# Forward transforms that fold mirrored time rows in a rotated basis, with the mirrored rows gathered by index and the row blocks normalised one at a time

## The chip, the cores and the metric

The kernel runs on one core of one Trainium2 chip. The metric is device time in microseconds (us) of one execution. A run counts as fast or slow by its distance from the fastest run of the same kernel (over 1.5% is slow), and comparisons below use fast runs alone.

Engine names are those of the profile: PE is the tensor engine, PEld its weight loads, DVE VectorE, ACT ScalarE, POOL GpSimd, SP the engine whose queue issues most DMA transfers.

## The reference, cut to what matters

```python
def _A_ref(q, k, v, shift_k, ssm_k, ssm_D):        # S = 2048 rows, D = 640 channels, bf16
    k_shift = sum over 4 taps t of k_pad[:, t:t + S, :] * shift_k[:, 3 - t]
    kv = k_shift * v
    y = irfft(rfft(kv, 2 * S) * rfft(ssm_k, 2 * S))[:S]   # causal convolution along time
    return q * (y + kv * ssm_D)

def _B_ref(x, w1, b1, w2, b2):
    h = _layernorm(x)                                # per row, over 640 channels
    u = gelu(einsum("bsd,sf->bdf", h, w1) + b1)      # F = 1536; contracts over time
    return transpose(einsum("bdf,fs->bds", u, w2) + b2)

g = sigmoid((q * gate_w).sum(-1))
out = g * _A_ref(q, k, v, ...) + (1 - g) * _B_ref(q, ...)
```

Both halves need the same `q`. Part B (the "MLP" below) is 2 x 384 matmuls of 320 columns. Part A is a convolution computed with forward transforms of `ssm_k` (called W, two halves of the time axis) and of `kv` (called A, two halves), a product, and inverse transforms. MLP matmuls have no partner that they must wait for once their rows of X are normalised, so the kernel uses them as filler on PE wherever part A makes PE wait.

## The kernel before

A small list scheduler written in the kernel orders every operation on its engine by a model of durations. `.after` adds an edge to that model only: it shapes the order and is not a wait at run time. Waits at run time come from the data that an operation reads and writes. `dma(..., chain=True)` puts transfers on the SP queue in the given order. `tt` and `ts` are tensor-tensor and tensor-scalar operations on the named engine, and `act` is an ACT operation that empties the PE accumulator into SBUF.

```python
        def k_turn(hk):                      # k rows -> transposed k, for the 4-tap shift
            o, i = kp[hk % 2], kn[hk % 2]
            # ... ov, iv: views that regroup channels
            SC.add("DVE", 0.75, ... tensor_copy(ov, iv) ..., prio=0, name="kperm")
            c0 = 16 + 128 * (hk % 2)
            dma(KT[hk // 2][:, :, c0:c0 + 128], o[:, :, :], ..., transpose=True, chain=True)
# ... loads and the transform basis: integer angles on DVE, Sin on ACT ...
        def fwd(src, h, p, dst, slot, scale, name, neg=...):     # 64 matmuls, 16 evictions per transform
            for k2 in range(2):
                for c in range(2):
                    # ...
                    for kt in range(2):
                        for ci in range(2):
                            items.append((chk(ci), FTB[:, p, kt, c, k2, :], src(kt, p, ci), kt == 0, kt == 1))
                    mms(vt, items, name=name)
                    act(o, two, ACT.Copy, vt=vt, name=name + "e", **kw)
# ... mixing: six DVE operations of 2560 to 5120 elements a transform ...
        def ln_apply():
            ts("POOL", sd[:, :], mv[:, :, 1], 1e-5, None, ALU.add)
            tt("POOL", rstd[:, :], sd[:, :], V(cst, 1, [[0, 16]]), ALU.pow)
            tt("POOL", sd[:, :], sd[:, :], rstd[:, :], ALU.mult)
            for t in range(16):
                xs = X[:, t // 4, t % 4, :]
                ts("DVE", xs, xs, mv[:, t, 0:1], rstd[:, t:t + 1], ALU.subtract, ALU.mult, mode=4, extra=0.16)
# ...
            if h == 0:
                # ... statistics of the 16 row tiles (ln_tile, DVE) ...
                ln_apply()
                for g0 in (0, 10):           # KF: the taps spread out, the other operand of the kv matmuls
                    tt("POOL", KF[:, g0:g0 + 10, :, :], V(cw, ...), V(m32, ...), ALU.mult)
                for hk in range(2):
                    k_turn(hk)
                mixing(C[0], SS, 0, fine=True)
            else:
                mixing(C[1], C[0], 0, conj=True)
# ... v loads, second pair of k rows, their k_turn, next w1 chunk: all on the SP queue in this order ...
        def v1mix(Wh, Ws, Vh, Vs):           # part of the mixing of W, done by accumulating transfers
            for i in range(2):
                dma(V(Vh, ...), V(Wh, ...), 128 * 5120 * 2, stream="POOL", prio=0, accum=True)
        v1mix(C[0], 2, C[1], 2)
        v1mix(SS, 0, C[0], 0)
# ... kv(hk): 40 matmuls KF x KT a quarter, ACT eviction, DVE product with v; then fwd of kv, mixing ...
```

## Time and profile before

| | before |
|---|---|
| time, median of 3 runs | 192.68 us (192.67 to 192.70) |
| span of the profiled run | 190.9 us |
| PE, DVE, ACT, POOL busy | 177.4, 170.3, 116.4, 33.0 us |
| PE idle (span less busy) | 13.5 us |
| X normalised (16 operations) | 30.05 to 35.84 us |
| first kv matmuls | 41.77 us |
| PE unbroken | from 51.75 us on |

From the page of the kernel before: engines with busy time, its share of the span and the number of instructions; two rows of the forty slices (a digit is the busy share of a slice in tenths; PEclk is the clock granted to PE); and the chain of waits that ended last.

```profile
PE 177.4 (93%) x1403; PEld 130.5 (68%) x1403; DVE 170.3 (89%) x195; ACT 116.4 (61%) x187; POOL 33.0 (17%) x29
PE   0749989999799999999999999999999999999993
...
PEclk9999999999999999999999999999999999999999
...
PE 71%; DVE 19%; DMA 4%; POOL 2%; issue 2%; SPq 0%; ACT 0%; DVEq 0%
PE pp L293 71%; DVE stats L845 6%; DMA X<-in_A_q_dram 4%; DVE X L628 3%; DVE SS L617 3%; DVE C L617 2%; DVE kp L724 2%; POOL rstd L617 2%; DVE vkv L617 1%; DVE mv L847 1%; POOL sd L627 1%; SPq L267 0%; ACT O L655 0%; DVE O L617 0%; DVEq L187 0%
```

PE is busy 93% of the time, the granted clock drops in no slice, and most of the chain is PE itself. What a change of the transforms can win must come out of PE's work or its idle 13.5 us.

The timeline of DVE and then of POOL before (start, duration, engine, line, operation, shapes, count, and in brackets the idle time before and its releaser).

```profile
21.58 0.82 DVE L724 COPY kp<-kn 128x2560 bf16<-128x2560 bf16 x1
...
24.56 0.83 DVE L724 COPY kp<-kn 128x2560 bf16<-128x2560 bf16 x1
...
30.05 5.79 DVE L628 TENSOR_SCALAR X<-X,mv,rstd 128x640 bf16<-128x640 bf16 x16 [3.19 <-POOL rstd L617]
```

```profile
13.65 7.84 POOL L617 TENSOR_TENSOR KF<-cw,m 128x2240 bf16<-128x2240 bf16 x2 [5.40 <-DVE mv L847]
25.60 1.39 POOL L627 TENSOR_SCALAR sd<-mv 128x16 f32<-128x16 f32 x1 [4.11 <-DVE mv L847]
27.07 2.94 POOL L617 TENSOR_TENSOR rstd<-sd,cst 128x16 f32<-128x16 f32 x1
```

Sixteen normalisations take 5.79 us.

Second, the SP queue and POOL's own transfers before.

```profile
48.19 6.34 SPq L260 DMA_TRANSPOSE KT<-kp  x2
```

### The profile page before, as it was taken

To read this page: it belongs to the slowest core of one execution; us is meant where nothing else is said; L and a number is where in the kernel's file an instruction comes from. 1 tells how busy PE (TensorE), PEld (TensorE's weight loads), DVE (VectorE), ACT (ScalarE), POOL (GpSimd) and SP (SyncE) were. 2 spreads that over 40 slices of the span, in tenths; PEclk is the share of its full clock that TensorE was granted. 3 is DMA by queue.
4 is the path that set the end of the run, shared out by engine and by line. 5 is a ranking of instruction groups with operands and counts; after the bars stand their busy time and mean duration, and the time that the engine had idled before them with its cause. 6 is when DMAs were issued, how large, how long until landed. Compare 5 with 4: busy or idle time off the path is not lost.

```text
span 190.9 us, 3358 instructions
## 1 busy us (share of the span) xinstructions
PE 177.4 (93%) x1403; PEld 130.5 (68%) x1403; DVE 170.3 (89%) x195; ACT 116.4 (61%) x187; POOL 33.0 (17%) x29
## 2 busy tenths in 40 slices
PE   0749989999799999999999999999999999999993
PEld 0536555678566976767777777888888777886782
DVE  7999967999999799999999969999999958999451
ACT  4799997889599999998411221131322467516632
POOL 2619563600006300010012102250000000000000
PEclk9999999999999999999999999999999999999999
DMA  5999999993799999994368914999947903210222
GB/s 155 327 412 378 372 238 230 307 407 136 136 181 306 250 232 306 272 329 96 59 138 251 231 27 138 272 208 195 263 136 224 367 18 137 72 69 2 72 103 103
DMA packets 37296, 38.93 MB, mean 204 GB/s; under 512 B 15644, under 2 KB 32673, under 8 KB 37281
## 3 DMA queue, kind: packets, MB, share of 16 engines
q1 hardware_dynamic: 34464, 32.15, 54.7%
q0 software_dynamic: 2752, 6.55, 18.6%
q8 instruction: 11, 0.18, 0.4%
q14 instruction: 5, 0.03, 0.0%
q10 hardware_dynamic: 64, 0.01, 0.0%
HBM read 25.87 MB, written 2.62 MB: 149 GB/s over the span
## 4 chain that ended last, share of the span: by engine, by line
PE 71%; DVE 19%; DMA 4%; POOL 2%; issue 2%; SPq 0%; ACT 0%; DVEq 0%
PE pp L293 71%; DVE stats L845 6%; DMA X<-in_A_q_dram 4%; DVE X L628 3%; DVE SS L617 3%; DVE C L617 2%; DVE kp L724 2%; POOL rstd L617 2%; DVE vkv L617 1%; DVE mv L847 1%; POOL sd L627 1%; SPq L267 0%; ACT O L655 0%; DVE O L617 0%; DVEq L187 0%
## 5 line engine op out<-in xcount | busy, mean ns | idle before, releaser
L293 PE MATMUL pp<-X,ring 128*128 128x320 bf16 x384 | 54.0, 299 | 0.1
L293 PE MATMUL pp<-GT,W 128*128 128x320 bf16 x384 | 52.8, 299 | 0.0
L617 DVE TENSOR_TENSOR C<-C 128x2560 bf16<-128x2560 bf16 (+1 forms) x28 | 48.9, 1769 | 1.2 <-ACT C L655 1.1
L293 PEld LDWEIGHTS pp<-GT,W 128*128 128x128 bf16 x384 | 43.5, 113 | 8.9 <-ACT cgb L655 0.2
L293 PEld LDWEIGHTS pp<-X,ring 128*128 128x128 bf16 x384 | 37.1, 98 | 15.4 <-DVE X L628 0.7
L655 ACT ACTIVATE C<-pp 128x640 bf16<-128x640 f32 x64 | 39.6, 741 | 4.4 <-PE pp L293 4.3
L655 ACT ACTIVATE O<-pp,c,omg 128x640 bf16<-128x640 f32 (+1 forms) x17 | 14.5, 853 | 32.9 <-PE pp L293 32.9
L655 ACT ACTIVATE GT<-pp,cc 128x640 bf16<-128x640 f32 x12 | 9.6, 797 | 22.1 <-PE pp L293 21.9
L617 DVE TENSOR_TENSOR tm<-C,C 128x2560 bf16<-128x2560 bf16 (+2 forms) x12 | 20.2, 1708 | 1.9 <-DMA C<-tm 1.9
L293 PE MATMUL pp<-wT,FTB 128*128 128x320 bf16 x128 | 19.6, 310 | 0.6 <-ACT wT L655 0.4
L655 ACT ACTIVATE cgb<-pp,gg 128x640 bf16<-128x640 f32 x16 | 12.7, 793 | 7.7 <-PE pp L293 7.7
L293 PEld LDWEIGHTS pp<-wT,FTB 128*128 128x128 bf16 x128 | 11.5, 101 | 8.0 <-ACT C L655 2.3
L617 DVE TENSOR_TENSOR C<-tm 128x2560 bf16<-128x2560 bf16 (+1 forms) x12 | 15.0, 1263 | 0.1
L293 PE MATMUL pp<-ident,ssm 128*128 128x128 bf16 x80 | 8.8, 265 | 6.6 <-DMA ssm<-in_A_ssm_k_dram 5.3
L262 POOL DMA_DIRECT2D C<-C x6 | 7.5, 1407 | 36.0 <-DVE C L617 36.0
L845 DVE BATCH_NORM_STATS2 stats<-X 128x6 f32<-128x320 bf16 x32 | 13.4, 463 | 0.3 <-DMA X<-in_A_q_dram 0.3
L293 PE MATMUL pp<-C,GTB 128*128 128x320 bf16 x96 | 13.6, 299 | 0.0
L293 PEld LDWEIGHTS pp<-ident,ssm 128*128 128x128 bf16 x80 | 6.3, 127 | 9.1 <-DMA ssm<-in_A_ssm_k_dram 5.3
L293 PEld LDWEIGHTS pp<-C,GTB 128*128 128x128 bf16 x96 | 9.0, 98 | 4.0 <-ACT O L655 0.2
L655 ACT ACTIVATE gq<-gq 128x640 bf16<-128x640 bf16 x16 | 11.8, 756 | 0.0
L617 DVE TENSOR_TENSOR tm<-C,SS 128x5120 bf16<-128x5120 bf16 x4 | 11.2, 2817 | 0.0
L655 ACT ACTIVATE wT<-pp 128x640 bf16<-128x640 f32 x16 | 10.1, 812 | 1.1 <-PE pp L293 1.1
(64 smaller groups left out, 177.2 us busy)
## 6 DMA issues: line engine op xcount, KB each, us to landing
ring<-in_B_w_dram SPq DMA_DIRECT2D x12, 512.0 KB, 10.3
W<-in_B_w_dram SPq DMA_DIRECT2D x8, 768.0 KB, 7.3
C<-C POOLq DMA_DIRECT2D x6, 640.0 KB, 10.5
ssm<-in_A_ssm_k_dram SPq DMA_DIRECT2D x4, 640.0 KB, 9.1
X<-in_A_q_dram SPq DMA_DIRECT2D x4, 640.0 KB, 9.5
kn<-in_A_k_dram SPq DMA_DIRECT2D x4, 640.0 KB, 9.2
out_dram<-O SPq DMA_DIRECT2D x7, 320.0 KB, 2.3
vkv<-in_A_v_dram SPq DMA_DIRECT2D x2, 640.0 KB, 4.7
```

Of the source, the lines that this page charges most:

```text
L262: ins = engobj.dma_start(out_ap, in_ap, accum_op=ALU.add, max_dma_last_dim=2560)
L293: ins = self.nc.tensor.matmul(ps_ap, lhsT=lhsT, rhs=rhs, start=start, stop=stop, skip_group_check=True)
L617: return SC.add(eng, d, lambda s: T.op(eng, lambda e: e.tensor_tensor(o, a, b, op), [a, b], [o]), [a, b], [o], prio=prio, name="tt")
L627: return e.tensor_scalar(o, a, s1, None, op0=op0)
L628: return e.tensor_scalar(o, a, s1, s2, op0=op0, op1=op1)
L655: return T.op("ACT", lambda e: e.activation(o, src, func, **kw), rr + [src], ww)
L724: SC.add("DVE", 0.75, lambda s: T.op("DVE", lambda e: e.tensor_copy(ov, iv), [i[:, :, :]], [o[:, :, :]]), [i[:, :, :]], [o[:, :, :]], prio ...
L845: SC.add("DVE", 0.38, (lambda o, i: lambda s: T.op("DVE", lambda e: e.bn_stats(o, i), [i], [o]))(o, i), [i], [o])
L847: SC.add("DVE", 0.12, (lambda o, i: lambda s: T.op("DVE", lambda e: e.bn_aggr(o, i), [i], [o]))(o, i), [i], [o])
```

## The change

Its intent is to do less. A time row and its mirror (row 1024 - n) meet the same cosine up to sign and the same sine up to sign. If the rows are first folded (sum and difference with the mirrored row), the second stage of the transform is partly done before the matmuls, so a transform needs 56 matmuls instead of 64 and the mixing on DVE loses two operations of 2560 elements. The price is that every second block of rows must arrive in reverse: `k` and `v` rows are gathered by an index, `ssm_k` is reversed by copies. The folds of W are done by accumulating signed transposes on PE, those of kv on DVE. The rotated basis is no longer its own transposed inverse, so the inverse basis is built again late (integer angles, Sin). And the normalisation is cut into four blocks so that MLP filler can begin sooner. The core of the diff, with cuts:

```diff
 # loads: odd blocks reversed by a gathered load issued from POOL
+        def block_load(t, off, src, h, e):
+            o = V(t, off, [[1, 4 * D]])
+            if e:
+                dma(o, dr(src, 0, [[4 * D, S // 4], [1, 4 * D]]), 128 * 5120, stream="POOL", rows=bidx[:, h:h + 1])
+            else:
+                dma(o, dr(src, 1024 * h * D, [[4 * D, 128], [1, 4 * D]]), 128 * 5120, chain=True)
 ...
+        for hk in range(1, 4):
+            w1_load(0, hk)
         for hk in range(2):
             k_load(hk)
-        for hk in range(4):
-            w1_load(0, hk)
 ...
+        def turn(h, d0, nd, eng="POOL"):      # reversal copies of ssm_k
+            o, i = ssmR[h][:, d0:d0 + nd, :, :], V(ssm, ... [[1024, nd], [1, 4], [-4, 128]])
+            return SC.add(eng, ..., tensor_copy(o, i), ..., name="turn")
 ...
-        def mixing(R, Th, Ts, fine=False, conj=False):
+        def mixing(R, Th, Ts, conj=False):
 ...
-            tt("DVE", sl(R, 2), sl(Th, Ts), sl(Th, Ts + 1), ALU.add)
-            tt("DVE", sl(R, 3), sl(Th, Ts), sl(Th, Ts + 1), ALU.subtract)
+            tt("DVE", sl(R, 2), sl(Th, Ts), sl(R, 3), ALU.add)
+            tt("DVE", sl(R, 3), sl(Th, Ts), sl(R, 3), ALU.subtract)
 ...
-        def ln_apply():
-            ts("POOL", sd[:, :], mv[:, :, 1], 1e-5, None, ALU.add)
-            tt("POOL", rstd[:, :], sd[:, :], V(cst, 1, [[0, 16]]), ALU.pow)
-            tt("POOL", sd[:, :], sd[:, :], rstd[:, :], ALU.mult)
-            for t in range(16):
+        def ln_scale(hk):
+            a, b = 4 * hk, 4 * hk + 4
+            ts("POOL", sd[:, a:b], mv[:, a:b, 1], 1e-5, None, ALU.add, prio=0)
+            tt("POOL", rstd[:, a:b], sd[:, a:b], V(cst, 1, [[0, 4]]), ALU.pow, prio=0)
+            return tt("POOL", sd[:, a:b], sd[:, a:b], rstd[:, a:b], ALU.mult, prio=0)
+
+        def ln_apply(hk):
+            for t in range(4 * hk, 4 * hk + 4):
 ...
-                ln_apply()
-                for g0 in (0, 10):
-                    tt("POOL", KF[:, g0:g0 + 10, :, :], ...)
+                    lnlast = ln_scale(hk)
+                    if hk:
+                        ln_apply(hk - 1)
+                ln_apply(3)
                 for hk in range(2):
                     k_turn(hk)
 ...
+        for g0 in (0, 10):
+            tt("POOL", KF[:, g0:g0 + 10, :, :], ...).after.update((turn1, lnlast))
 ...
-                    128 * 5120 * 2, stream="POOL", prio=0, accum=True)
+                    128 * 5120 * 2, stream="POOL", prio=0, accum=True).after.update(kturns)
 ...
-        for p in range(4):
-            dma(GTB[...], FTB[...], 128 * 2048, rate=200.0, transpose=True, prio=10 ** 5)
+        for p in (0, 2, 1, 3):                # inverse basis: 16 integer operations, 4 masks, 4 Sin
+            ...
```

## The prediction

> **What bounds the kernel now.** The tensor engine. The page gives PE 177.4 of 190.9 us busy; DVE 170.3, ACT 116.4. The chain of waits is one unbroken PE run from 51.75 to 187.81 us; before 51.75 it runs through DVE (normalisation statistics, a wait for GpSimd's power, mixing). The timeline shows MLP matmuls filling every gap from 30.64 us on, when the first of X is normalised. PE's "busy" before that is partly padding: the first 64 W-transform matmuls take 10.29 us (161 ns each, against 137 to 141 ns for MLP ones) because each group of four waits for a 0.60 us ACT eviction; 35 transposes take 3.96 us (113 ns) at the pace of 0.63 us evictions, though five weight loads take 0.32 us (64 ns). At 64 ns a transpose and 138 ns a 320-column matmul, PE needs about 15.5 us of work between 5.3 and 30.6 us: some 10 us is recoverable, plus a 1.04 us wait for the kv product at 50.7.
>
> **What the change does (estimates from those durations).**
> - Transforms: 64 to 56 matmuls each, four transforms: 32 x 0.14 = 4.5 us less PE.
> - W transposes: 80 to 140 (folding by accumulated signed transposes): +60 x 0.064 = 3.8 us. PE demand: about -0.7 us net.
> - ACT evictions: same number (64 + 16), so the W stage stays bound by ACT until about 41 us. Fewer matmuls there only make room for MLP filler.
> - DVE: mixing loses two 2560-element operations per transform, -8 x 1.4 = 11 us. Added: folds of kv about 2 x 2.1; the inverse basis built by 16 integer operations and four masks, about 6.7; reversal copies and small items about 2.5. Forward angles: about -1. Net -1 to +2 us busy, but the 3.2 us DVE wait for the power (idle before X) goes.
> - GpSimd: gains reversal copies, four normalisation chains, three halo copies (the one now took 2.9 us), gathered loads[...]. Its chain ts 1.39, power 2.94, multiply 0.22 may shrink little with size, so four could cost 10 to 18 us.
> - ACT: four late Sin calls (1.15 us each) among Gelus need table loads (1.28 each in this trace[...]). ACT waits 3.5 us per Gelu there, so little harm. Four basis transposes by DMA go.
>
> **On the critical path.** The gain is not the fewer matmuls but normalised X arriving by blocks (estimate 17, 22, 27, 32 us instead of all by 35.8), so MLP filler uses PE while ACT evicts: 4 to 5 us of the 10. The first transposes wait for the reversal, about 1 to 2 us lost. Late, inverse matmuls end at 180.02 with 7.8 us of MLP filler left, so DVE doesn't bind if its net is as above; PE savings reach the end.
>
> **Predicted: 188.0 us, 80% range 184.0 to 192.5.** Chances: faster by over 2% 0.57, within 2% 0.37, slower 0.06.
>
> **Checks.** PE busy 172 to 176; first MLP matmul before 25 us; W stage still ends near 41; no PE gap after 52 us; inverse transforms ending well before the last MLP matmuls; table loads 4 to 8.
>
> **What would make it wrong.** GpSimd: if its queue holds up the second transpose or the power, PE idles before 30 us and the gain vanishes. Gathered loads are issued by GpSimd[...]; GpSimd-issued accumulations here took 10 to 18 us to land against 9 for ordinary loads, so late k or v rows could starve the kv stage beyond the MLP filler of the first weight chunk. Or the inverse basis comes late and table loads stall Gelu's eviction. On the other side, near-perfect filling would give about 184.

## More of the kernel before

The two KF products on POOL (13.65 to 21.49) run beside the statistics, not beside the normalisations.

```profile
57.02 2.64 POOL L262 DMA_DIRECT2D C<-C  x2 [19.65 <-DVE C L617]
61.34 2.43 POOL L262 DMA_DIRECT2D C<-SS  x2 [1.68 <-DVE C L617]
```

The second pair of k transposes is issued from 48.19 to 54.53 us; the accumulating transfers of W's mixing come after it, from 57.02 us. The k transposes land in 4.9 to 9.7 us, with a median of 5.0: this second pair in 5.0 and 4.9, and the 9.7 is the first transpose of all, issued at 22.42 us while w1 loads are still in flight.

## The result and the profile after

The ratios below are the mean time of one kernel's fast runs over the mean of the other's fast runs of the same rounds, so they are not quite the ratio of the quoted medians.

| | before | after |
|---|---|---|
| time, median | 192.69 us (192.67 to 192.75) | 205.44 us (202.65 to 207.62) |
| ratio of fast runs | 1 | 1.0577, interval 1.0474 to 1.068 |
| span of the profiled (fast) run | 190.9 us | 202.8 us |
| PE busy, PE idle | 177.4, 13.5 us | 179.8, 23.0 us |
| DVE, ACT, POOL busy | 170.3, 116.4, 33.0 us | 183.1, 130.9, 43.3 us |
| last of X normalised | 35.84 us | 41.58 us |
| first kv matmuls | 41.77 us | 53.05 us |
| PE unbroken from | 51.75 us | 95.38 us |

The kernel is 5.8% slower; as two of its four runs count as slow by the 1.5% rule, this rests on the other two (202.65 and 204.98 us, mean 203.8). The span grew by 11.9 us: 9.5 us more PE idle time (23.0 less 13.5) and 2.4 us more PE busy time (179.8 less 177.4), although PE has less to do. By PE's waits, the 9.5 us are mainly 4.7 us for X and 2.6 us for the halo copies (edge columns of k that POOL copies next to their neighbours), neither of which PE waited for before, then about 1 us more at the start and 0.9 us more for the kv product. The page of the kernel after, the same lines as before:

```profile
PE 179.8 (89%) x1431; PEld 133.2 (66%) x1431; DVE 183.1 (90%) x234; ACT 130.9 (65%) x198; POOL 43.3 (21%) x51
PE   1199999289996994989999999999999999999993
...
PEclk9999999958998899999999999999999999999999
...
PE 52%; DVE 25%; DMA 10%; ACT 8%; POOL 3%; issue 2%; SPq 0%; POOLq 0%; DVEq 0%
PE pp L296 52%; DVE X L640 7%; DVE stats L895 6%; DMA KT<-kp 5%; DMA kn<-in_A_k_dram 5%; ACT gq L667 3%; DVE C L629 3%; DVE pint L640 3%; ACT ksh L667 2%; ACT C L667 1%; DVE vkv L629 1%; POOL KT L952 1%; DVE mv L897 1%; DVE ssmR L827 1%; DVE kp L744 1%
```

A slice is 5.07 us. PE has a new hole around 36 to 41 us (digit 2), after which the clock falls to half for a slice, and smaller ones at 62 to 64 us (digit 6; the clock dips again) and 76.7 to 79.6 us (digit 4). Three names on the chain are new or larger: "DVE X" at 7% (3% before), and "DMA KT<-kp" and "DMA kn" at 5% each (absent before). The first two turned out to be the causes; the third follows from the first, as is shown below. The timeline of DVE after, then of POOL:

```profile
18.42 3.36 DVE L640 TENSOR_SCALAR X<-X,mv,rstd 128x640 bf16<-128x640 bf16 x1
...
30.71 0.81 DVE L744 COPY kp<-kn 128x2560 bf16<-128x2560 bf16 x1
...
32.81 8.77 DVE L640 TENSOR_SCALAR X<-X,mv,rstd 128x640 bf16<-128x640 bf16 x4 [0.58 <-POOL rstd L629]
41.50 1.48 DVE L629 TENSOR_TENSOR SS<-C 128x2560 bf16<-128x2560 bf16 x1
...
44.42 0.82 DVE L744 COPY kp<-kn 128x2560 bf16<-128x2560 bf16 x1
```

```profile
18.96 2.62 POOL L827 COPY ssmR<-ssm 128x1536 bf16<-128x1536 bf16 x2
...
33.00 8.04 POOL L629 TENSOR_TENSOR KF<-cw,m 128x2240 bf16<-128x2240 bf16 x2
```

The last four normalisations take 8.77 us where four took 1.45 before (5.79 for 16). In the same 8 us POOL does its two KF products, 4.02 us each, and the slowest single normalisation of the run took 4.07 us. In the first block already, a normalisation of 3.36 us lies beside the reversal copies on POOL. The chain of waits then goes on: mixing at 41.50, and the k copy that began at 24.56 before now begins at 44.42. PE during this:

```profile
37.29 0.45 PE L296 MATMUL pp<-X,ring 128*128 128x320 bf16 x2 [1.13 <-DVE X L640]
41.28 1.25 PE L296 MATMUL pp<-X,ring 128*128 128x320 bf16 x4 [3.54 <-DVE X L640]
...
63.98 3.73 PE L296 MATMUL pp<-vkv,FTB 128*128 128x320 bf16 x14 [1.97 <-DVE vkv L629]
```

The four matmuls at 41.28 take as long as eight do elsewhere (1.25 us): the granted clock was 0.50 from 41.28 to 46.5 us (0.66 in the whole stretch 40 to 50 us). Before it lie 4.67 us of waits in 36 to 41.3 us, 3.54 of them in one piece. A shorter wait was followed by half clock too: after the 1.97 us before 63.98 the granted clock was 0.52 from 64 to 66 us, and the 14 matmuls there took 266 ns each; and in e13 (below), after one of 2.52 us, eight matmuls took 1.78 us and the next six 1.80. The waits of 1.49 and 1.15 us before 78.14 and 79.57 us were not followed by it: the granted clock was 1.00 from 79.57 to 90 us. What decides it was not isolated.

The SP queue after, and POOL's transfers:

```profile
31.54 16.67 SPq L261 DMA_TRANSPOSE KT<-kp  x2
...
48.88 0.43 SPq L270 DMA_DIRECT2D kn<-in_A_k_dram  x1
...
59.65 11.70 SPq L261 DMA_TRANSPOSE KT<-kp  x2
```

```profile
56.67 1.32 POOL L265 DMA_DIRECT2D C<-C  x1 [3.86 <-DVE C L629]
62.73 1.22 POOL L265 DMA_DIRECT2D C<-C  x1 [4.74 <-DVE C L629]
69.88 2.42 POOL L265 DMA_DIRECT2D C<-SS  x2 [5.93 <-DVE C L629]
77.24 2.27 POOL L952 COPY KT<-KT 128x20 bf16<-128x20 bf16 x2 [4.95 <-DMA KT<-kp]
```

The queue waits for the late k copy from 31.54 on, so the rows of the second half are issued at 48.88 (before: 34.18), and their transposes at 59.65. DVE, with the next k copy in its order, stood 2.44 us until these rows had landed at 58.8 us; behind that copy came the kv product that PE waited 1.97 us for. The accumulating transfers now come in the middle of the transposes, and the second pair takes 7.2 and 10.0 us to land (5.0 and 4.9 before). From 76.7 us PE stands still, but for two matmuls, for the halo copies behind it, until 79.57 us. From 95.38 us on PE is as unbroken as before; all of the loss is earlier.

### The profile page after: what moved, and what is told of

Read it like the earlier page. It is cut to its first block, busy times and chain, and to the rows that moved or that the text cites. A ratio compares the mean times of both kernels' runs of the same rounds, so it can differ in the third digit from the quotient of the medians.

```text
span 202.8 us, 3488 instructions
## 1 busy us (share of the span) xinstructions
PE 179.8 (89%) x1431; PEld 133.2 (66%) x1431; DVE 183.1 (90%) x234; ACT 130.9 (65%) x198; POOL 43.3 (21%) x51
## 4 chain that ended last, share of the span: by engine, by line
PE 52%; DVE 25%; DMA 10%; ACT 8%; POOL 3%; issue 2%; SPq 0%; POOLq 0%; DVEq 0%
PE pp L296 52%; DVE X L640 7%; DVE stats L895 6%; DMA KT<-kp 5%; DMA kn<-in_A_k_dram 5%; ACT gq L667 3%; DVE C L629 3%; DVE pint L640 3%; ACT ksh L667 2%; ACT C L667 1%; DVE vkv L629 1%; POOL KT L952 1%; DVE mv L897 1%; DVE ssmR L827 1%; DVE kp L744 1%
## 5 line engine op out<-in xcount | busy, mean ns | idle before, releaser
L296 PE MATMUL pp<-X,ring 128*128 128x320 bf16 x384 | 57.4, 304 | 4.7 <-DVE X L640 4.7
L296 PEld LDWEIGHTS pp<-GT,W 128*128 128x128 bf16 x384 | 43.3, 114 | 9.2 <-ACT cgb L667 0.4
L667 ACT ACTIVATE C<-pp 128x640 bf16<-128x640 f32 x64 | 40.5, 726 | 7.9 <-PE pp L296 7.7
L629 DVE TENSOR_TENSOR C<-C 128x2560 bf16<-128x2560 bf16 x21 | 31.1, 1486 | 2.3 <-ACT C L667 2.1
L296 PE MATMUL pp<-wT,FTB 128*128 128x320 bf16 x112 | 18.3, 315 | 0.3 <-ACT C L667 0.3
L640 DVE TENSOR_SCALAR X<-X,mv,rstd 128x640 bf16<-128x640 bf16 x16 | 16.3, 1060 | 0.6 <-POOL rstd L629 0.6
L296 PEld LDWEIGHTS pp<-wT,FTB 128*128 128x128 bf16 x112 | 10.6, 103 | 6.7 <-ACT C L667 2.0
L629 DVE TENSOR_TENSOR C<-C,C 128x2560 bf16<-128x2560 bf16 (+1 forms) x12 | 15.0, 1263 | 0.0
L667 ACT ACT_TABLE_LOAD x10 | 12.8, 1283 | 2.5 <-issue 2.3
L667 ACT ACTIVATE gq<-gq 128x640 bf16<-128x640 bf16 x16 | 11.9, 760 | 0.5 <-DVE gq L629 0.5
```

Source lines behind the costliest of these rows:

```text
L296: ins = self.nc.tensor.matmul(ps_ap, lhsT=lhsT, rhs=rhs, start=start, stop=stop, skip_group_check=True)
L629: return SC.add(eng, d, lambda s: T.op(eng, lambda e: e.tensor_tensor(o, a, b, op), [a, b], [o]), [a, b], [o], prio=prio, name="tt")
L640: return e.tensor_scalar(o, a, s1, s2, op0=op0, op1=op1)
L667: return T.op("ACT", lambda e: e.activation(o, src, func, **kw), rr + [src], ww)
```

## The experiments

Two theories came out of the traces. **P** (for POOL): POOL instructions keep DVE's normalisations (and copies) out while they run; KF beside the last block is the main case. **T** (for transposes): k transposes are slow when accumulating transfers are in flight with them. The rivals were **K**, that the k rows simply are issued too late, and that the changed transforms themselves cost more. In the edits below, "after" and "before" name the kernel that was edited.

### P: KF beside the normalisation

**e1**, after: the KF products get a real dependency on the last normalised tile.

```diff
-            tt("POOL", KF[...], V(cw, ...), V(m32, ...), ALU.mult).after.update((turn1, lnlast))
+            rd_ = [ka, kb_, X[:, 3, 3, :]]
+            SC.add("POOL", 4.78, ... tensor_tensor(ko, ka, kb_, ALU.mult), rd_, [ko] ...)
```

> The changed kernel (205.4 us) with the two GpSimd products for KF made to wait for the last normalisation of X. Theory P[...] the last four normalisations took 8.77 us instead of 1.5. Held, they take about 1.5 us, X is complete near 34.5 us instead of 41.6, TensorE's 4.7 us wait for X and the half clock that followed go, the second row turn for the k transpose moves from 44.4 to under 40 us; total 195 to 199 us. Rival K (late k rows: the load order put them behind three weight loads): the total stays within 2 us of 205.

Measured: 217.66 us, ratio 1.128. The time was missed by far, and the mechanism hit. The timeline of DVE, then of POOL, of e1:

```profile
32.81 1.52 DVE L640 TENSOR_SCALAR X<-X,mv,rstd 128x640 bf16<-128x640 bf16 x4 [0.58 <-POOL rstd L629]
34.24 1.49 DVE L629 TENSOR_TENSOR SS<-C 128x2560 bf16<-128x2560 bf16 x1
35.76 5.11 DVE L629 TENSOR_TENSOR C<-C 128x2560 bf16<-128x2560 bf16 x1
40.80 4.56 DVE L744 COPY kp<-kn 128x2560 bf16<-128x2560 bf16 x1
```

```profile
34.71 9.97 POOL L932 TENSOR_TENSOR KF<-cw,m 128x2240 bf16<-128x2240 bf16 x2
```

Without KF beside them the four normalisations take 1.52 us. KF then held up whatever DVE did next: a mixing operation of 1.49 us took 5.11 and a copy of 0.82 us took 4.56. The wait only moved, and the slowest k transpose took 26.1 us to land, which put a 14.0 us hole into PE. What was held in these two kernels, each time by 3.6 to 3.7 us beside one KF product of 4 to 5 us: the tensor_scalar normalisations after the change (4.07 us at the slowest, against 0.36), and the tensor_tensor and the copy of e1. By what means POOL holds them was not shown.

**e2**, after: KF cleared at the start by POOL, the products a tenth of their size (the error stayed within the tolerance). Its output is wrong, which doesn't matter for the time.

```diff
+        memset("POOL", KF[:, :, :, :], 0.0)
-            tt("POOL", KF[:, g0:g0 + 10, :, :], ...)
+            tt("POOL", KF[:, g0:g0 + 1, :, :], ..., dur=4.78)      # the model's duration kept
```

> Wrong result on purpose: the changed kernel, every engine's order kept, but each KF product on GpSimd computes one group of ten (the rest is zeroed at the start), so it is about a tenth as long. Theory P: the last four normalisations take 1.5 to 2.5 us instead of 8.77 and the total falls to 195 to 199 us, like the kernel with KF held. Rival K: within 2 us of 205.

Measured: 203.61 us, ratio 1.0515. The last four normalisations took 2.00 us, but the clearing itself held the first angle operations on DVE (three of them 5.13 us instead of 0.68), and everything started 3.7 us later. The run is confounded and says only that here a POOL operation that reads nothing, the clearing of 3.82 us from 1.97 us on, held tensor_scalar operations.

**e5**, after: the same small products, the rest of KF filled by a load instead, the order on every engine unchanged. Its output is wrong, which doesn't matter for the time.

```diff
+        dma(V(KF, 0, [[1, 4480]]), dr(A_k, 0, [[10240, 128], [1, 4480]]), 64, chain=True)
-            tt("POOL", KF[:, g0:g0 + 10, :, :], ...)
+            tt("POOL", KF[:, g0:g0 + 1, :, :], ..., dur=4.78)
```

> Wrong result on purpose, and a mend of the run with KF zeroed, whose zeroing itself held VectorE at the start: the changed kernel in the same order on every engine, but each KF product is a tenth as long and the rest of KF comes by one load from HBM in a quiet stretch of DMA. Theory P[...]: the last four normalisations take at most 2.5 us instead of 8.8, X is complete by 35.5 us instead of 41.6, TensorE does not wait for X more than 1 us after 35 us, total 196 to 200 us. If the total stays over 202 although the normalisations are short, a second cause holds the kernel, and the long landing of the second pair of k transposes (10 us in the changed kernel, 23 us with KF held) is the first suspect.

Measured: 197.52 and 197.69 us (fast) and 200.98 and 200.99 us (slow). Against the after kernel's fast 202.65 and 204.98 us, taking POOL's 8 us of KF away saves 5 to 7 us. The last four normalisations took 2.00 us, and the second k copy stood at 37.59 instead of 44.42:

```profile
32.74 2.00 DVE L640 TENSOR_SCALAR X<-X,mv,rstd 128x640 bf16<-128x640 bf16 x4 [0.57 <-POOL rstd L629]
```

PE no longer waits for X. This is the cleanest size of P, and it is not the whole loss: 5 us over the kernel before remain.

**e3**, the kernel before: KF moved to the same place, right after the power, beside the sixteen normalisations.

```diff
-                ln_apply()
+                lnlast = ln_apply()
-                    tt("POOL", KF[...], ...)
+                    tt("POOL", KF[...], ...).after.add(lnlast)
```

> The kernel before with only the two KF products moved on GpSimd's queue, from before the normalisation statistics' end to right after the power, so that they run beside the 16 normalisations. Theory P: the 16 normalisations stretch from 5.8 to 11 us or more, and the kernel slows by 3 to 8 us (196 to 201). Rival K, and any theory in which the folded transforms themselves are the cause: normalisations stay near 5.8 us and the total within 1.5 us of 192.7.

Measured: 200.56 us, ratio 1.0416 (1.0386 to 1.0446). One moved pair of POOL operations makes the kernel before 4.2% slower: the 16 normalisations took 13.05 us (before: 5.79), as KF ran from 30.50 to 38.51, and PE waited 6.5 us for X.

```profile
30.27 13.05 DVE L628 TENSOR_SCALAR X<-X,mv,rstd 128x640 bf16<-128x640 bf16 x16 [3.19 <-POOL rstd L617]
```

```profile
30.50 8.01 POOL L617 TENSOR_TENSOR KF<-cw,m 128x2240 bf16<-128x2240 bf16 x2
```

P needs none of the new transforms.

**e7**, the kernel before with only the block-wise normalisation of the change (its diff is the `ln_scale`/`ln_apply` part above).

> The kernel before with only the block-wise normalisation of the change. Theory P: KF's products and the early normalisations now share the same stretch, the first four or eight normalisations are stretched to 1 to 4 us each, and what the earlier start wins is lost again: 191 to 197 us. If blocks are good by themselves (my prediction's view), 187 to 190 us.

Measured: 192.45 us, ratio 0.9982 (0.9965 to 0.9999). The first MLP matmul came at 27.77 us instead of 30.64, and this bought 0.2%. Two limits of the run show. The second KF product fell between the blocks (20.75 to 24.69) and held one normalisation for 3.75 us. And the first four normalisations were done at 20.73, but this run keeps the old order of loads: the first quarter of w1, which an MLP matmul needs as well, was issued at 12.81 us and landed 11.0 us later, near 23.8 (the change issues it at 2.96). So the 64 W matmuls from 14.46 to 25.79, the stretch that filler was to use, got none of it. By 50 us PE had done 354 matmuls against 359 before. What blocks are worth when neither KF nor w1 is in the way was not run.

### K: are the k rows too late?

**e4**, after: the first k rows ahead of the last three quarters of the first w1 chunk on the SP queue.

```diff
-        for hk in range(1, 4):
-            w1_load(0, hk)
         for hk in range(2):
             k_load(hk)
+        for hk in range(1, 4):
+            w1_load(0, hk)
```

> The changed kernel with the first k rows loaded before the last three quarters of the first weight chunk, as the kernel before did. Rival K: the first k transpose is issued before 27 us instead of 31.5, the kv convolution starts by 46 us instead of 53, and the total falls to 199 or less. Theory P: VectorE is still held until 41.6 us, the second k turn stays near 44 us, and the total stays within 2 us of 205.

Measured: 202.69 us, ratio 1.0505. The first transposes are issued 5 us earlier (26.8 against 31.5), the waits for X stay (4.5 us), and the time is within the spread of the after kernel. K as the main cause falls (e12 against e10, further down, says the same: 193.35 and 193.31 us).

**e8**, e4 with the second k copy ahead of the first mixing on DVE.

```diff
-                mixing(C[0], SS, 0)
+                mixing(C[0], SS, 0).after.add(kperm[1])       # plus the bookkeeping for kperm
```

> The changed kernel with the first k rows loaded early and VectorE's second k turn put ahead of the first mixing. If the late second k turn (it holds the sync engine's queue with the v and k loads behind it) matters by itself, the second pair of k transposes is issued about 3 us earlier than in the run with k rows first and the total falls from 202.7 to 198 to 200.5 us. Theory P alone: VectorE is held to 41.6 us all the same, total within 1.5 us of 202.7.

Measured: 218.51 us, ratio 1.1363. An earlier k copy made the kernel slower by 16 us: the slowest k transpose took 24.8 us to land, and PE waited 18.2 us at once for the halo copy behind it. This and e6 are what T was formed from.

### T: transposes beside accumulating transfers

**e6**, after: normalisation in one piece again, KF under the statistics again, so that P is gone.

```diff
-                    lnlast = ln_scale(hk)
-                    if hk:
-                        ln_apply(hk - 1)
-                ln_apply(3)
+                ts("POOL", sd[:, :], mv[:, :, 1], 1e-5, None, ALU.add)
+                tt("POOL", rstd[:, :], sd[:, :], V(cst, 1, [[0, 16]]), ALU.pow)
+                tt("POOL", sd[:, :], sd[:, :], rstd[:, :], ALU.mult)
+                for hk in range(4):
+                    ln_apply(hk)
+                for g0 in (0, 10):
+                    tt("POOL", KF[...], ...)                   # and its later place removed
```

> The changed kernel with one part undone: X is normalised in one piece after all statistics, and KF's products fall where the kernel before had them, under the statistics. Theory P: no normalisation is stretched (16 in 5.8 to 7 us), X is complete by 37 us, total 192 to 197 us. Rival F (the folded transforms, gathers and halo copies are the loss, not the blocks): total 199 us or more, with X complete by 37 us all the same.

Measured: 212.19 us, ratio 1.0994. The normalisations are as quick as before (6.0 us for 16, though complete only at 40.4 us, not 37), and yet it lost about 8 us more (fast runs against fast runs). This is the outcome that rival F, the new transforms, had forecast; e10 below takes it away from F. The k transposes of e6 as the trace sums them up, and its rows of the forty slices (5.27 us each):

```profile
DMA to landing us min/median/max: 6.0/9.8/20.4
```

```profile
PE   1199978999989103997999999999999999999994
...
PEclk9999999999999955799699999999999999999999
```

The transposes were issued from 54.57 to 66.87 us, the first accumulating transfers at 51.98 and 54.11. PE is idle for some 13 us between 69 and 83 us and its clock falls to half (granted 0.50 from 75 to 85 us). The waits show the way there: the kernel keeps gate products (`gq`) in the memory of one of the two k copies, so DVE's next gate product waited 16.99 us until the transpose had landed, and ACT and then PE waited behind it (PE 13.29 us).

**e9**, after: the four accumulating transfers wait, by a real semaphore, for the second pair of transposes.

```diff
+        if hold is not None:
+            self.do_waits(stream, self.deps_for(stream, [(r, "R") for r in self.regions(hold)]))
-            ..., stream="POOL", prio=0, accum=True).after.update(kturns)
+            ..., stream="POOL", prio=0, accum=True, hold=V(KT[1], 0, [[1, NG * KTW]])).after.update(kturns)
```

> The changed kernel with the four accumulating loads of the W mixing made to wait until the second pair of k transposes has landed. Theory T[...]: the slowest k transpose lands in 7.5 us or less instead of 10, but the halo copies still queue behind the four issues on GpSimd, so the gain is small: total 201 to 205 us against 205.4. Rival (transposes are slow for another cause, such as their own queue): landing unchanged.

Measured: 207.00 us, ratio 1.0742. The transposes landed in at most 6.6 us (10.0 before the edit), as T says. But the halo copies, which need the same transposes, stood behind the four issues on POOL's queue, and PE waited 4.2 us for them. The total missed its range (201 to 205): the hold alone costs the changed kernel some 3 us.

**e10**, e6 with the hold and with the halo copies ahead of the accumulating transfers.

```diff
-        v1mix(C[0], 2, C[1], 2)
-        v1mix(SS, 0, C[0], 0)
         halo(kcol(0, 272), kcol(0, 143))
         halo(kcol(1, 15), kcol(0, 144))
         halo(kcol(1, 272), kcol(1, 143))
+        v1mix(C[0], 2, C[1], 2)               # with hold=..., as in e9
+        v1mix(SS, 0, C[0], 0)
```

> The run with normalisation in one piece (212.2 us, slowest k transpose 20.4 us to landing) with the accumulating loads held until the second pair of k transposes has landed, and the halo copies ahead of them. Theory T: slowest k transpose 7.5 us or less, TensorE's gap from 70 to 80 us gone, total 194 to 199 us. Rival: transposes still over 12 us, total over 206.

Measured: 193.31 us, ratio 1.002 (1.0003 to 1.0037). It takes 18.9 us off e6 and brings the folded transforms level with the kernel before, a little better than its range. The second pair of transposes of e10, issued from 54.40 us:

```profile
DMA to landing us min/median/max: 5.0/5.0/5.1
```

In e6 this pair took 10.7 and 20.4 us. The slowest of e10 at 8.8 us, over the 7.5 expected, is the first transpose of all, which meets other loads (among them the gathered v rows, issued at 28.10 and 34.37 us) and no accumulating transfer (8.9 us in e6; 9.7 in the kernel before, beside w1 loads). What the hold and the new order of the halo copies do apart was not measured here.

**e11**, e8 with the same hold and halo order (its edit is that of e10 on e8).

> The run with the second k turn ahead of the first mixing (218.5 us, slowest k transpose 24.8 us) with the same hold and halo order. Theory T: slowest k transpose 7.5 us or less, total 196 to 201 us[...]. Rival: total over 210.

Measured: 196.99 us, ratio 1.0205 (1.0185 to 1.0226), 21.5 us less than e8; the slowest transpose took 6.5 us instead of 24.8. What remains is P: the block-wise normalisations still took 16.4 us and PE waited 4.5 us for X.

**e14**, e6 with the four accumulating transfers as plain copies. Its output is wrong, which doesn't matter for the time.

```diff
-                    ..., stream="POOL", prio=0, accum=True).after.update(kturns)
+                    ..., stream="POOL", prio=0).after.update(kturns)
```

> Wrong result on purpose: the run with normalisation in one piece and nothing held (212.2 us, slowest k transpose 20.4 us), with the four accumulating loads of the W mixing turned into plain copies of the same bytes from the same queue. If only accumulation slows the transposes, the slowest lands in 8 us or less and the total is under 200; if any such traffic in flight slows them, they stay over 12 us and the total over 206.

Measured, one run of unknown state: 199.89 us; the second pair of transposes landed in 6.8 and 9.2 us instead of 10.7 and 20.4. With the same issue times, most of the delay goes with the accumulation; the plain copies still cost something over the 5 us that the pair takes without them (e10). The outcome lies between the two that were expected.

**e15**, the kernel before: the second pair of k copies held until the W mixing of the second half is done, so that its transposes meet the accumulating transfers.

```diff
+            rd_ = [i[:, :, :]] + ([V(C[1], 2 * SL, [[1, 2 * SL]])] if hk > 1 else [])
-            SC.add("DVE", 0.75, ... tensor_copy(ov, iv), [i[:, :, :]], [o[:, :, :]], ...)
+            SC.add("DVE", 0.75, ... tensor_copy(ov, iv), rd_, [o[:, :, :]], ...)
```

> The kernel before with the second pair of k turns held back until the W mixing of the second half is done, so that their transposes meet the accumulating loads as in the changed kernel. Theory T: the slowest k transpose goes from 5 to 10 us or more to landing, and the total rises by 4 to 20 us. Rival: the transposes stay at 5 to 6 us and the total rises by less than 3 us, as MLP work fills the delay.

Measured: 203.90 us, ratio 1.0581 (1.0566 to 1.0596), by chance the loss of the change itself. The k transposes of e15, and who waited for them:

```profile
  PE pp L293: 8.7, 1
...
DMA to landing us min/median/max: 4.9/7.7/19.3
```

The transposes were issued from 57.36 us and the accumulating transfers at 58.37 and 61.17. Some of the 11 us is plain lateness, since the copies were held; the 19.3 us against 5 is not. T, too, needs none of the new transforms.

### What is left when both causes are removed

**e12**, e10 with the k rows of e4.

```diff
 # e10, and:
+        for hk in range(2):
+            k_load(hk)
         for hk in range(1, 4):
             w1_load(0, hk)
-        for hk in range(2):
-            k_load(hk)
```

> Both causes removed at once, result correct: normalisation in one piece with KF under the statistics, accumulating loads held, halo copies first, and the first k rows loaded early. [...]189 to 195 us, near or below the kernel before (192.7). If the folded transforms bring a cost of their own, 196 us or more.

Measured: 193.35 us, ratio 1.002. Correct, free of P and T but for small rests (the first k copy took 1.33 us instead of 0.82), PE busy for 175.3 us (2.1 less than before), and still no gain. Two waits of the start explain it in the trace: PE has its first reversed rows at 10.62 us (the kernel before begins its transposes at 5.34), and X begins to be normalised at 33.64 us instead of 30.05. In the timeline of e10 the power on POOL stands behind the reversal copies (24.05 to 27.93) and behind a gathered load, whose issue took POOL 2.11 us.

**e13**, e12 with the reversal copies earlier on DVE and POOL, KF after them, and the gathered v loads after the power.

```diff
-            return SC.add(eng, ..., name="turn")
+            return SC.add(eng, ..., prio=0, name="turn")
-                dma(o, ..., stream="POOL", rows=bidx[:, h:h + 1])
+                dma(o, ..., stream="POOL", rows=bidx[:, h:h + 1]).after.update(lnl)     # lnl: the power's chain
+        for g0 in (0, 10):
+            tt("POOL", KF[...], ..., prio=0).after.add(turn1)
```

> The run with both causes removed (193.35 us), and its start mended: the reversal copies ahead of the last angles on VectorE and ahead of KF on GpSimd, and the gathered v loads after the normalisation's power. If the transforms' fewer matmuls and mixings (PE busy 175.3 us against 177.4) are only eaten by the later start (TensorE waits for the reversal until 10.6 us, X normalised from 34.2 us), the first W transposes finish 2 us earlier, X is normalised from about 29 us, and the total is 188 to 191.5 us, below both kernels. If something else eats them, 192.5 us or more.

Measured over five rounds: 195.89 us, ratio 1.0173 (1.0131 to 1.0216). A miss, and the trace says why. The first transposes came at 7.45 us as meant, but with k loaded early the first k copy was now scheduled among the statistics on DVE. It waited for its rows until 23.50 us and then ran beside KF (2.13 us instead of 0.82). The statistics ended near 29.7 us and X still began at 34.32.

**e16**, the same without e4's order of loads, so that the first k copy falls after the statistics; that is e10 with e13's edit.

> The one-piece, held version (e10, 193.31 us) with the reversal copies earlier on VectorE and GpSimd and the KF products after them; the first k rows stay where the changed kernel has them, so that the first k turn falls after the statistics and not among them, as it did in e13. If the later start of the W transposes (first one at 10.6 us against about 5 before) is what eats the 2 us of tensor-engine time that the fold saves: first transposes before 8 us, statistics done by 26 us, first X normalisation by 31.5, and 189.5 to 191.9 us. If the start does not matter, because the stage waits for X, ACT or k in any case: 192.5 to 194. Above 195 would mean that the KF products or the power again meet something on VectorE.

Measured over five rounds: 191.41 us median (five fast runs of 190.60 to 192.09, one slow of 197.43), ratio 0.9929 (0.991 to 0.9949). It lies in the expected range, and beats the kernel before by 0.7% (clear of noise) and the change by about 6% (191.2 against 203.8 us, means of fast runs of different rounds). From the page and the timelines of e16:

```profile
PE 175.5 (93%) x1431; PEld 130.4 (69%) x1431; DVE 172.7 (91%) x234; ACT 130.0 (69%) x198; POOL 39.5 (21%) x42
PE   0498999999899999899999999999999999999993
```

```profile
30.78 4.15 DVE L642 TENSOR_SCALAR X<-X,mv,rstd 128x640 bf16<-128x640 bf16 x11 [2.08 <-POOL rstd L631]
```

```profile
16.82 7.88 POOL L631 TENSOR_TENSOR KF<-cw,m 128x2240 bf16<-128x2240 bf16 x2
26.27 1.45 POOL L641 TENSOR_SCALAR sd<-mv 128x16 f32<-128x16 f32 x1 [1.57 <-DVE mv L901]
27.80 2.94 POOL L631 TENSOR_TENSOR rstd<-sd,cst 128x16 f32<-128x16 f32 x1
```

The first transposes are at 7.20 us instead of 10.63, X starts at 30.78 instead of 33.61 (e10), and KF lies under the statistics, which it doesn't hold up (a pair of them took 0.83 us beside it). Mending the start wins the two microseconds back (e10's fast runs have a mean of 193.4 us). How much is due to the transposes and how much to X was not separated: the edit moves both.

## Why the prediction was wrong

The prediction said 188.0 us, with 184 to 192.5, and gave 0.06 to what happened. Point by point:

- **The failed step** is "normalised X arriving by blocks (estimate 17, 22, 27, 32 us instead of all by 35.8), so MLP filler uses PE while ACT evicts: 4 to 5 us of the 10". The blocks were complete at 21.8, 26.6, 32.2 and 41.6 us, and PE, instead of gaining 4 to 5 us, waited 4.7 us for X. The estimate took a normalisation at its 0.36 us (5.79 over 16) whatever POOL did; the change put the KF products right behind the last scale, and each of them kept one normalisation out for about its full 4 us (the slowest took 4.07 us beside products of 4.02; e1, e3, e5). The first three blocks were about 5 us late as well: the statistics began at 10.49 us instead of 8.77, and POOL's reversal copies held a normalisation of the first block for 3.36 us. The risk was named for POOL's queue and for gathered loads, and not for DVE's own operations. The first MLP matmul did come before 25 us, as forecast (20.92), and didn't save it. Whether blocks would bring the 4 to 5 us without the collision stays open: in the kernel before they brought 0.2% (e7), with one KF product and late w1 rows in the way.
- **"No PE gap after 52 us" failed** for a cause that the prediction did not have: the DMA queue. It did fear late k rows, from gathered loads. The gathered k loads landed in 8.6 us (median), no later than the 9.2 us of ordinary k loads before (the two ordinary ones after took 11.0). But ordinary late k rows had their part: the load issued at 48.88 us, behind the late k copy on the SP queue, held DVE for 2.44 us. What was slow beyond that were the transposes, once the delay of the k copies had moved them among the accumulating transfers (T: e6 against e10, e8 against e11, and e15 in the kernel before).
- **The rest is clock.** PE busy time was to fall to 172 to 176 us; it rose to 179.8 as PE ran at half clock after two waits (3.54 us before 41.28 and 1.97 us before 63.98; granted 0.50 and 0.52). The estimate from the trace: some 5.7 and 3.5 us at half clock are 4.6 us lost, which leaves 175.2. Where the gaps are gone it is 175.0 to 175.5 (e10, e12, e16): the PE term of the sum was right in sign, a little too careful (2 us instead of 0.7).
- **GpSimd's four scale chains** were guessed at 10 to 18 us. The four powers took 1.05 to 1.08 us each, against 2.94 for the one of 16 columns, and the four chains together 7.0 us (1.9 for the additions, 4.3 for the powers, 0.8 for the products). That guess was too high; the danger was elsewhere.
- **"W stage still ends near 41"**: it ended at 52.1 us. From 36 to 41 us PE, which took its matmuls in the program's order, stood in front of MLP matmuls whose rows of X were not there, and the W matmuls stood behind them.
- **Late table loads** did no harm, as predicted, though they were ten and not 4 to 8: 1283 ns each, and PE unbroken from 95.38 us.
- **"The first transposes wait for the reversal, about 1 to 2 us lost"** was mis-sized. They began at 10.63 us for the reversed rows, some 5 us later than before, and this together with the late power on POOL is what kept e10 and e12 from gaining (e16).

What stays open: why accumulating transfers slow a transpose. In e6's slices from 58 to 79 us the transfer engines are counted at least 90% busy while moving 128 to 195 GB/s, against 345 to 398 GB/s in its first full slices, so the profile counts them as occupied while little arrives; e14, one run, ties most of it to the accumulation. The mechanism was not isolated, nor was the number of transfers at which it begins. The landing of a transpose of 640 KB, side by side: about 5 us where no load or accumulating transfer was in its way (e10, second pair), 6.8 and 9.2 us beside four plain copies issued from POOL (e14, one run), 9.7 us beside w1 loads (the first one of the kernel before), 10.7 and 20.4 us beside the same four as accumulating transfers (e6), and 24.8 and 26.1 us at worst (e8, e1). P and T also don't add up neatly: against the fast runs of the change (mean 203.8 us), shrinking KF saved 5 to 7 us (e5), undoing the blocks cost 8 (e6, through T), removing T alone cost 3 (e9, through the halo copies), and removing both saved 10 (e10).

## What to carry to other kernels

Before moving an operation on GpSimd, look at what VectorE does in that stretch: here a product of 4 to 5 us placed beside 0.4 us normalisations, a copy or a two-input operation cost VectorE 3.6 to 3.7 us (the changed kernel, e1), while statistics beside it lost nothing (440 to 494 ns for each of the 32 of the kernel before; a pair took 0.83 us before its 7.8 us of KF products began and 0.83 to 0.84 beside them). When a change delays a producer, follow the DMA queue to its end: the later transfers may meet traffic that they never met before (here the second pair of transposes took 7.2 and 10.0 us to land instead of 5.0 and 4.9), and an order in a scheduler's model is no wait at run time. And when a change that saves work gains nothing, first remove its collisions one by one and together, as single repairs can each make it slower.
